# Two attention blocks, forward and backward on one core: how O, dQ, dwo and dwq work is placed, in which order stores are issued, and how the first head's K is transposed

## The chip, the cores and the metric

The kernel runs on one core of a Trainium2 chip. A core has TensorE (matmuls, and transposes done as matmuls against an identity), VectorE, ScalarE, GpSimd and SyncE, each with an instruction queue of its own, and DMA queues. The metric is the time of one execution on the device in microseconds (us).

## The reference

Two independent attention blocks, A and B, get the same shapes: batch 8, 96 queries, 32 heads of 128, 512 cached keys and values, model width 640. The program returns the forward result and all gradients, in bf16:

```python
q = (x @ wq).reshape(B, Sq, H, Dh)          # B=8 Sq=96 D=640 H=32 Dh=128
scores = einsum("bhqd,bhkd->bhqk", q, k_cache) * Dh ** -0.5      # Sk=512
o = einsum("bhqk,bhkd->bhqd", softmax(scores), v_cache)
out = o.reshape(B, Sq, H * Dh) @ wo         # of A and of B, side by side
# reference() returns out and the gradients of x, k_cache, v_cache, wq, wo of both blocks
```

With P the softmax and O the head's output, the backward pass needs per head: dO = g wo^T, dV = P^T dO, dP = dO V^T, dS = P (dP - rowsum(O dO)), dK = dS^T Q, dQ = dS K, dwo = O^T g, dwq = x^T dQ, dx = dQ wq^T.

## The kernel before

The work is cut into **ticks**. Each block has 32 heads, each head 8 batch elements, and each (head, batch element) pair starts one tick after the one before; so a head takes 8 ticks, a block 256. `build_block` (line 54) adds closures to an `Emitter` (line 16) with a tick and a slot; `Emitter.run` sorts them by tick, slot and order of adding, and calls them. That gives the program order. The framework's scheduler may still move an instruction ahead or back within its engine's queue, by readiness as it reckons it and by program order as priority. An instruction that goes through `pinned` (line 111) stays behind the one that was traced before it on its engine.

In what follows an offset is counted in ticks from a pair's own first tick (`ct`), or from its head's first tick (`c0t`).

**A pair's stages** (table `OFF`, line 45). K and V come from memory for two batch elements at a time, on SyncE's queue (`c_ld`, lines 262 to 270). V is transposed by DMA (`c_xt`, line 275). K is transposed by DMA for the batch elements 2, 3, 6, 7 (two at a time, issued at offset -3) and on TensorE for 0, 1, 4, 5 (`c_s1`, line 280, at offset 2: four transposes and a VectorE copy to `KT_pe`); `k_on_pe` (line 548) chooses. At offset 3 the scores S and their row maximum (lines 298, 300), the exponential on ScalarE (line 310), the reciprocal (line 320) and, on GpSimd, P = E / sum (`P_sb`, line 329, pinned). At offset 4 the transposes of P into the bank `x_ps` (line 365) and dV (line 389), evacuated by ScalarE (line 392). At 5 O^T (line 359), evacuated to the tile `OD` (line 375), and on GpSimd O * dO (`prod`, line 407, pinned). At 6 dP and the row sums `dl_ps` (lines 417, 419), then dS on VectorE (line 421). At 7 the transposes of dS (line 346) and dK (line 432), evacuated by ScalarE (line 435). At 8 dQ^T (line 340).

**Stores** of dV and dK go out on GpSimd's queue for two batch elements together (`c_st`, line 395; the issue is line 398), one tick after the second one's evacuation, in a slot behind P_sb and prod of that tick. They are not pinned. The tiles `dV_sb` and `dK_sb` have three buffers each.

**A head's own work** is placed by the table `HK` (line 46): transposes of wo and wq (`pB`), the projections Q^T and dO^T (`pC`), their transposes back (`pD`), and after the pairs:

- `qA` (line 438): transposes of O^T (which = 0) and dQ^T (which = 1) into `Onat` and `dQnat`, six each, evacuated by VectorE; O at offset 18, dQ at 17
- `qB` (line 459): dwo in two halves of 320 columns, six matmuls each (line 470), offsets 19 and 20, evacuated by ScalarE to `dwo_sb`; with the second half the store is issued on GpSimd's queue (line 474)
- `qD` (line 477): dwq for two heads at a time, with the odd one, in five blocks of 128 rows and 6 matmuls of 256 columns each (line 490); two blocks share a bank and a VectorE evacuation at offsets 18 and 19, the fifth comes at 21; the store of `dwq_sb` is line 496

`Onat`, `dQnat`, `dwo_sb` and `dwq_sb` have one buffer each. O^T and dQ^T of the last eight heads lie in `OD`. The last head of the second block has offsets of its own.

**A group's work**: for every five or six heads `gU` (line 501) adds their share of out and of dx, spread over some nine ticks each; line 512 has its matmuls.

**Between the blocks**: the second block's x and gradient are loaded in 12 pieces (`setup_ld`, line 114, pinned on SyncE's queue), through a pool of five buffers. The last seven can be loaded only when an earlier piece has been transposed (`setup_T`, line 122) and its buffer is free; they are transposed themselves in ticks -4 to -1 of the second block. They are loaded again in natural layout (`setup_nat`, line 138) for dwo and dwq, from ticks 13 (gradient) and 15 (x), into the tiles that the first block's dwo and dwq still read until then.

Of the kernel before, what the change touches and what calls it, by code (L numbers as in the profile page):

```python
# [13 lines left out]


class Emitter:
    def __init__(self):
        self.items = []
        self.n = 0

    def add(self, tick, slot, fn):
        self.items.append((tick, slot, self.n, fn))
        self.n += 1

    def run(self):
        self.items.sort(key=lambda x: (x[0], x[1], x[2]))
# [14 lines left out]
SL_HEAD = 90  # L41
SL_GRP = 95
SL_SETUP = 96

OFF = dict(ldk=-5, ldv=-3, kt=-3, vt=0, s2=3, s3=3, s4=4, s5=5, s6=6, s7=7, s8=8)
HK = dict(pA=-10, pA2=-9, pB=-3, pC0=[-2, 0], pC1=[-1, 0], pD1=1, pD0=2, qA0=18, qA1=17, qB=[19, 20], qD=[(18, 0, 2), (19, 2, 4), (21, 4, 5)])
EV = dict(pB0="act", pB1="dve", pC00="act", pC01="act", pC10="act", pC11="dve", pD0="dve", pD1="dve", qA0="dve", qA1="dve", qB0="act", qB1="act", qD="dve", gU="act")
GSPREAD0 = 9
PRIO_OFF = 2000
# [4 lines left out]
def build_block(tc, em, tick0, blk, x, kc, vc, wq, wo, g_all, out_all, dx, dk, dv, dwq, dwo, ident, ones, pools, HG=6, first=True, groups=None):  # L54
    nc = tc.nc
# [116 lines left out]
    if first:  # L172
        for which_, tk in ((0, -12), (1, -11)):
            em.add(tick0 + tk, SL_LOAD + which_, setup_nat(which_, 0, 4))
            em.add(tick0 + tk, SL_LOAD + which_, setup_nat(which_, 4, TT))
    else:
        for which_, tk in ((1, 13), (0, 15)):
            for i, t in enumerate(range(0, TT, 2)):
                em.add(tick0 + tk + i // 2, SL_LOAD, setup_nat(which_, t, min(t + 2, TT)))

# [99 lines left out]
    def c_s1(h, b):  # L280
        def f():
            st = CS[(blk, h, b)]
            kT_ps = bank([128, Sk], BF16, "kT_ps")
            for c in range(KC):
                nc.tensor.transpose(kT_ps[:, c * 128:(c + 1) * 128], st["K_sb"][:, c, :], ident[:])  # L285
            KT = wk.tile([128, Sk], BF16, name="KT_pe", bufs=2)
            nc.vector.tensor_copy(KT[:], kT_ps[:])
            st["KT"] = KT[:]
        return f
# [105 lines left out]
    def c_st(h, b, which):  # L395
        def f():
            dst = dv if which == "v" else dk
            nc.gpsimd.dma_start(dst[b - 1:b + 1, h].rearrange("b (p c) d -> p b (c d)", c=KC), SB.pop((blk, h, b // 2, which))[:])  # L398
        return f

    def c_s5b(h, b):
# [144 lines left out]
    NTS = len(tsplits)  # L546

    def k_on_pe(h, b):
        return (b // NB) % 2 == 0

    SX = pools["SX"]
    for g in range(NG):
        h0 = GH0[g]
        for hh in range(groups[g]):
            h = h0 + hh
            c0t = tick0 + h * B
            if not (first and h == 0):
                em.add(c0t + HK["pA"], 54.6, pA(h))
                em.add(c0t + HK["pA2"], 54.6, pA2(h))
            em.add(c0t + HK["pB"], SL_HEAD, pB(h))  # L560
            fh = first and h == 0
            for si in range(NTS):
                em.add(c0t + HK["pC0"][min(si, len(HK["pC0"]) - 1)], SL_HEAD, pC(h, 0, si))
                em.add(c0t + (3 if fh else HK["pC1"][min(si, len(HK["pC1"]) - 1)]), SL_HEAD + (7 if fh else 0), pC(h, 1, si))
            em.add(c0t + (3 if fh else HK["pD1"]), SL_HEAD + (8 if fh else 0), pD(h, 1))
            em.add(c0t + (4 if fh else HK["pD0"]), SL_HEAD, pD(h, 0))
            for b in range(B):
                ct = c0t + b
                if b % NB == 0:
                    em.add(tick0 - 12 if first and h == 0 and b == 0 else ct + OFF["ldk"], SLOTS["LOAD"], c_ld(h, b, "K", 7))  # L570
                    em.add(ct + OFF["ldv"], SLOTS["LOAD"], c_ld(h, b, "V", 5))
                    if not k_on_pe(h, b):
                        em.add(ct + OFF["kt"], SLOTS["LOAD"] + 1, c_xt(h, b, "KT", 2))
                    em.add(ct + OFF["vt"], SLOTS["LOAD"] + 1, c_xt(h, b, "VT", 4))
                if k_on_pe(h, b):
                    em.add(ct + 2, SLOTS["S1"], c_s1(h, b))
                em.add(ct + OFF["s2"], SLOTS["S2A"], c_s2a(h, b))
                em.add(ct + OFF["s2"], SLOTS["S2B"], c_s2b(h, b))
                em.add(ct + OFF["s3"], SLOTS["S3A"], c_s3a(h, b))
                em.add(ct + OFF["s3"], SLOTS["S3B"], c_s3b(h, b))  # L580
                em.add(ct + OFF["s5"], SLOTS["S5B"], c_s5b(h, b))
                if b % 2 == 1:
                    em.add(ct + OFF["s4"] + 1, 54.3, c_st(h, b, "v"))
                    em.add(ct + OFF["s7"] + 1, 54.3, c_st(h, b, "k"))
                em.add(ct + OFF["s4"], SLOTS["S4"], c_s4(h, b))
                for i, o in enumerate(("s8", "s7", "s5", "s4")):
                    SX.setdefault(ct + OFF[o], [None] * 4)[i] = (blk, h, b)
                em.add(ct + OFF["s6"], SLOTS["S6"], c_s6(h, b))
                em.add(ct + OFF["s7"], SLOTS["S7"], c_s7(h, b))
            hk = HK if first or h < H - 1 else dict(HK, qA0=13, qB=[14, 15], qA1=16, qD=[(19, 0, 2), (19, 2, 4), (19, 4, 5)])  # L590
            em.add(c0t + hk["qA0"], SL_HEAD, qA(h, 0))
            for di in range(len(wsplits)):
                em.add(c0t + hk["qB"][di], SL_HEAD + 1, qB(h, di))
            em.add(c0t + hk["qA1"], SL_HEAD, qA(h, 1))
            for (k_, c_lo, c_hi) in hk["qD"]:
                if c_lo < DC and h % 2 == 1:
                    em.add(c0t + k_, SL_HEAD + 2, qD(h, c_lo, min(c_hi, DC)))
        cLg = tick0 + (h0 + groups[g] - 1) * B + B - 1
        gs0 = max(3, (GSPREAD0 * groups[g]) // HG)
        gs1 = max(3, (GSPREAD1 * groups[g]) // HG)  # L600
        if not first and g == NG - 2:
            gs0, gs1 = 9, 9
        if g == 0:
            em.add(cLg + OFF["s5"] - 2, SL_LOAD, setup_acc)
        subs = [(0, t, gi) for t in range(TT) for gi in range(len(gsplits))] + [(1, t, gi) for t in range(TT) for gi in range(len(gsplits))]
        n_out = TT * len(gsplits)
        for i, (which, t, gi) in enumerate(subs):
            if which == 0:
                tk = cLg + OFF["s5"] + 2 + (i * gs0) // n_out
            else:  # L610
                tk = cLg + OFF["s8"] + 2 + gs0 - 3 + ((i - n_out) * gs1) // n_out
            em.add(tk, SL_GRP, gU(g, which, t, gi))
    pools["c_s45"] = c_s45
    pools["c_s8"] = c_s8
    return tick0 + H * B
# [2 lines left out]
def _kernel_impl(tc, A_x, A_k_cache, A_v_cache, A_wq, A_wo, B_x, B_k_cache, B_v_cache, B_wq, B_wo, grad_out,  # L618
# [13 lines left out]
    with ExitStack() as ctx:  # L632
# [36 lines left out]
        for tk, (k8, k7, k5, k4) in pools["SX"].items():  # L669
            em.add(tk, SLOTS["S8"], pools["c_s8"](tk, k8, k7))  # L670
            em.add(tk, SLOTS["S5"], pools["c_s45"](tk, k8, k5, k4))
        em.run()


# [62 lines left out]
```

## Time and profile before

| | |
|---|---|
| median of 5 runs | 1716.59 us (1706.99 to 1733.63) |
| profiled execution | 1706.99 us, span 1705.2 us |
| TensorE matmul / weight load busy | 1678.3 us (98%) / 1341.7 us (79%) |
| VectorE / ScalarE / GpSimd busy | 1321.9 (78%) / 1381.9 (81%) / 1046.5 us (61%) |
| DMA | 424.66 MB, mean 249 GB/s |
| mean granted TensorE clock | 0.998 of full |

The page comes from one execution. The span runs from the first to the last instruction; the execution's own time is 1.8 us more. A row of a group has the line, the engine, the operation, the tiles written and read, and the count; then the time busy, the mean of one in ns, and the idle time of the engine just before, with what ended it. A row of waits has who waited for whom, then the total, the number and the longest in us. A row of the timeline has start and duration in us, and in square brackets the idle time before and its releaser. A row of windows has the stretch, its length, and then the busy time of each engine with its instructions in brackets; behind that the granted TensorE clock, the DMA share (the packets' time over 16 engines' time, which goes over 1 where packets wait in line) and GB/s. A matmul's end is modelled, so a wait below some 0.2 us can be missing from the idle time.

### The profile page before, as it was taken

What the parts mean: (1) busy time and instruction counts of PE and PEld (TensorE: products, weight loads), DVE (VectorE), ACT (ScalarE), POOL (GpSimd) and SP (SyncE); (2) the same over time, 40 slices, a digit from 0 to 9 for tenths busy, and PEclk for the clock granted to TensorE, in tenths of its full rate; (3) what the DMA queues carried; (4) which work ended last, traced back from release to release, by engine and by line L of the source; (5) the groups of instructions that cost most, each with busy time, mean ns of one, the idle gap of its engine ahead of it and who ended that gap; (6) DMA issues with size and microseconds to landing.
All of it is one profiled execution on the core that took longest, in us unless ns stands there. A gap on an engine that the chain in (4) does not pass through costs nothing.

```text
span 1705.2 us, 57281 instructions
## 1 busy us (share of the span) xinstructions
PE 1678.3 (98%) x21976; PEld 1341.7 (79%) x21976; DVE 1321.9 (78%) x3040; ACT 1381.9 (81%) x3518; POOL 1046.5 (61%) x1747
## 2 busy tenths in 40 slices
PE   8999999999999999999899999999999999999999
PEld 7787778778878778878678777887788778778876
DVE  6787678778778878788778776787788788778777
ACT  7899799778869869869768897897799679868974
POOL 4676466556657657657566665675577557656754
PEclk9999999999999999999999999999999999999999
DMA  9999999989999999999999999999999999989994
GB/s 268 252 269 274 253 235 283 254 198 262 245 234 249 263 235 253 250 250 269 261 255 245 276 274 243 250 243 262 235 266 259 243 227 271 282 199 246 262 233 132
DMA packets 606770, 424.66 MB, mean 249 GB/s; under 512 B 425696, under 2 KB 564320, under 8 KB 606496
## 3 DMA queue, kind: packets, MB, share of 16 engines
q1 hardware_dynamic: 552912, 243.65, 72.4%
q0 software_dynamic: 53584, 177.35, 31.7%
q8 instruction: 172, 2.82, 0.7%
q14 instruction: 102, 0.84, 0.2%
HBM read 161.09 MB, written 159.12 MB: 188 GB/s over the span
## 4 chain that ended last, share of the span: by engine, by line
PE 89%; DMA 4%; ACT 2%; POOL 2%; issue 2%; DVE 1%; DVEq 0%; SPq 0%; POOLq 0%; ACTq 0%
PE o_ps L512 12%; PE q_ps L243 12%; PE dK_ps L432 6%; PE dV_ps L389 6%; PE S_ps L298 6%; PE dwq_ps L490 6%; PE dP_ps L417 6%; PE dwo_ps L470 6%; PE x_ps L365 5%; PE x_ps L340 5%; PE dst_ps L346 5%; PE x_ps L359 5%; PE kT_ps L285 3%; PE n_ps L258 3%; PE nat_ps L455 3%; DMA KT<-K_sb 2%
## 5 line engine op out<-in xcount | busy, mean ns | idle before, releaser
L329 POOL TENSOR_SCALAR P_sb<-E_sb,rinv 96x512 bf16<-96x512 bf16 x512 | 352.0, 688 | 379.6 <-DVE rinv L320 369.9
L310 ACT ACTIVATE E_sb<-S_ps,negm 96x512 bf16<-96x512 f32 x512 | 354.9, 693 | 210.0 <-DVE negm L300 197.8
L421 DVE SCALAR_TENSOR_TENSOR dS_sb<-dP_ps,dl_ps,P_sb 96x512 bf16<-96x512 f32 x512 | 383.1, 748 | 65.4 <-PE dl_ps L419 49.1
L300 DVE TENSOR_REDUCE negm<-S_ps 96x1 f32<-96x512 f32 x512 | 347.7, 679 | 55.1 <-PE S_ps L298 51.8
L435 ACT ACTIVATE dK_sb<-dK_ps 128x512 bf16<-128x512 f32 x512 | 307.0, 600 | 67.2 <-PE dK_ps L432 62.6
L392 ACT ACTIVATE dV_sb<-dV_ps 128x512 bf16<-128x512 f32 x512 | 316.2, 618 | 0.0
L398 POOL DMA_DIRECT2D out_dram<-dV_sb x256 | 193.7, 757 | 134.3 <-ACT dV_sb L392 125.3
L378 ACT ACTIVATE PT_sb<-x_ps 128x384 bf16<-128x384 bf16 x512 | 257.7, 503 | 1.1 <-PE x_ps L365 1.1
L398 POOL DMA_DIRECT2D out_dram<-dK_sb x256 | 192.6, 752 | 84.3 <-ACT dK_sb L435 53.7
L512 PEld LDWEIGHTS <-OD 128*128 128x128 bf16 x1536 | 132.1, 98 | 99.8 <-issue 0.2
L389 PE MATMUL dV_ps<-dOnat_h,P_sb 96*128 96x128 bf16 x2048 | 198.2, 219 | 1.0 <-DVE dOnat_h L160 0.8
L417 PE MATMUL dP_ps<-VT,dOT_h 128*96 128x512 bf16 x512 | 195.5, 382 | 2.9 <-DMA VT<-V_sb 2.8
L432 PE MATMUL dK_ps<-Qnat_h,dS_sb 96*128 96x128 bf16 x2048 | 197.9, 219 | 0.0
L407 POOL TENSOR_TENSOR prod<-OD,dOT_h 128x96 bf16<-128x96 bf16 x512 | 186.0, 363 | 9.1 <-ACT OD L375 5.2
L348 DVE COPY dST_sb<-dst_ps 128x384 bf16<-128x384 bf16 x512 | 177.3, 346 | 9.2 <-PE dst_ps L346 7.9
L320 DVE RECIPROCAL rinv<-rowsum 96x1 f32<-96x1 f32 x512 | 79.5, 155 | 125.4 <-ACT E_sb L310 119.8
L365 PE MATMUL x_ps<-ident,P_sb 96*128 96x96 bf16 x2048 | 172.3, 205 | 4.3 <-POOL P_sb L329 3.1
L375 ACT ACTIVATE OD<-x_ps 128x192 bf16<-128x192 f32 (+1 forms) x515 | 172.5, 335 | 4.4 <-PE x_ps L340 3.8
L359 PE MATMUL x_ps<-PT_sb,V_sb 128*128 128x96 bf16 x2048 | 172.1, 206 | 0.4 <-ACT PT_sb L378 0.4
L346 PE MATMUL dst_ps<-ident,dS_sb 96*128 96x96 bf16 x2048 | 172.0, 206 | 0.5 <-DVE dS_sb L421 0.5
L340 PE MATMUL x_ps<-dST_sb,K_sb 128*128 128x96 bf16 x2048 | 170.6, 206 | 0.4 <-ACT PT_sb L378 0.4
L340 PEld LDWEIGHTS <-K_sb 128*128 128x128 bf16 x2048 | 131.5, 98 | 25.1 <-issue 1.0
(83 smaller groups left out, 3717.7 us busy)
## 6 DMA issues: line engine op xcount, KB each, us to landing
out_dram<-dV_sb POOLq DMA_DIRECT2D x256, 256.0 KB, 5.0
out_dram<-dK_sb POOLq DMA_DIRECT2D x256, 256.0 KB, 5.0
K_sb<-in_A_k_cache_dram SPq DMA_DIRECT2D x128, 256.0 KB, 5.2
V_sb<-in_A_v_cache_dram SPq DMA_DIRECT2D x128, 256.0 KB, 5.0
K_sb<-in_B_k_cache_dram SPq DMA_DIRECT2D x128, 256.0 KB, 4.8
V_sb<-in_B_v_cache_dram SPq DMA_DIRECT2D x128, 256.0 KB, 5.1
out_dram<-dwo_sb POOLq DMA_DIRECT2D x63, 160.0 KB, 4.9
out_dram<-dwq_sb POOLq DMA_DIRECT2D x31, 320.0 KB, 5.8
```

The costliest lines, as they stand in the source:

```text
L300: nc.vector.tensor_reduce(negm[:], S_ps[:], axis=AX.X, op=ALU.max, negate=True)
L310: nc.scalar.activation(E_sb[:], st["S_ps"][:], ACT.Exp, bias=st["negm"][:], scale=1.0, accum_out=rowsum[:])
L329: pinned(nc.gpsimd.tensor_scalar(P_sb[:], st["E_sb"][:], st["rinv"][:], 0.0, op0=ALU.mult, op1=ALU.add))
L340: nc.tensor.matmul(dQT_ps, st["K_sb"][:, c, :], st["dST_sb"][:, c * Sq:(c + 1) * Sq], start=(c == 0), stop=(c == KC - 1))
L389: nc.tensor.matmul(dV_ps[:, c * 128:(c + 1) * 128], P_sb[:, c * 128:(c + 1) * 128], hs["dOnat_h"][:, b * 128:(b + 1) * 128], start=True, s ...
L392: nc.scalar.activation(SB[(blk, h, b // 2, "v")][:, b % 2], dV_ps[:], ACT.Identity, scale=1.0)
L398: nc.gpsimd.dma_start(dst[b - 1:b + 1, h].rearrange("b (p c) d -> p b (c d)", c=KC), SB.pop((blk, h, b // 2, which))[:])
L417: nc.tensor.matmul(dP_ps[:], hs["dOT_h"][:, tok], st["VT"], start=True, stop=True)
L421: nc.vector.scalar_tensor_tensor(dS_sb[:], dP_ps[:], dl_ps[:, 0:1], st["P_sb"][:], op0=ALU.subtract, op1=ALU.mult)
L432: nc.tensor.matmul(dK_ps[:, c * 128:(c + 1) * 128], dS_sb[:, c * 128:(c + 1) * 128], hs["Qnat_h"][:, b * 128:(b + 1) * 128], start=True, s ...
L435: nc.scalar.activation(SB[(blk, h, b // 2, "k")][:, b % 2], dK_ps[:], ACT.Identity, scale=1.0)
L512: nc.tensor.matmul(o_ps[:], src[:, t * 128:(t + 1) * 128], rhs, start=(hh == 0), stop=(hh == groups[g] - 1))
```

## The change

The emitter gets a second way to add work. `later` takes an earliest and a latest tick, a slot, a number of TensorE columns and a gap (the least number of ticks behind the entry before it); entries keep their order in one chain over both blocks. All other work is booked with its columns per tick. `place` first gives every entry its earliest possible tick, then goes backward through the chain, up to 60 times, and moves an entry between its neighbours to the tick that lowers the sum of squared columns most; it stops when nothing moves.

The transposes `qA`, the halves of `qB` and the blocks of `qD` of all heads go through `later`, but for the last two heads of the second block, which keep fixed offsets. In the chain an odd head's work follows the even head's: O transposes, dwo halves, and with the odd head both dQ transposes and then dwq in five pieces, each with a bank and an evacuation of its own. An entry may be up to 58 ticks behind its head's first tick; the first block's work must end by tick 14 of the second block. The natural-layout loads of the second block move from ticks 13 and 15 to 15 and 17, and its dwo begins no earlier than tick 19.

The stores of dV and dK are pinned. For the first head of the first block all eight K go through TensorE, and its two transposing DMAs of K are left out.

```diff
 class Emitter:
...
-    def add(self, tick, slot, fn):
+    def add(self, tick, slot, fn, cols=0):
         self.items.append((tick, slot, self.n, fn))
         self.n += 1
+        self.cols[tick] = self.cols.get(tick, 0) + cols
+
+    def later(self, lo, hi, slot, fn, cols, gap=0):
+        self.chain.append([lo, hi, slot, fn, cols, gap])
+
+    def place(self):
+        ch = self.chain
+        at = []
+        for i, (lo, hi, _, _, cols, gap) in enumerate(ch):
+            t = max(lo, at[-1] + gap) if at else lo
+            at.append(t)
+            self.cols[t] = self.cols.get(t, 0) + cols
...
+        for _ in range(60):
+            moved = False
+            for i in reversed(range(len(ch))):
+                lo, hi, _, _, cols, gap = ch[i]
+                a = max(lo, at[i - 1] + gap) if i else lo
+                z = min(hi, at[i + 1] - ch[i + 1][5]) if i + 1 < len(ch) else hi
+                best, bt = 0, at[i]
+                for t in range(a, z + 1):
+                    if t != at[i]:
+                        d = (self.cols.get(t, 0) + cols) ** 2 + (self.cols[at[i]] - cols) ** 2 - self.cols.get(t, 0) ** 2 - self.cols[at[i]] ** 2
+                        if d < best:
+                            best, bt = d, t
+                if bt != at[i]:
+                    self.cols[at[i]] -= cols
+                    self.cols[bt] = self.cols.get(bt, 0) + cols
+                    at[i] = bt
+                    moved = True
+            if not moved:
+                break
+        for t, (_, _, slot, fn, _, _) in zip(at, ch):
+            self.add(t, slot, fn)
...
+QHOLD = 58
+QEND = 14
+QPIECES = [(0, 1), (1, 2), (2, 3), (3, 4), (4, 5)]
...
-        for which_, tk in ((1, 13), (0, 15)):
+        for which_, tk in ((1, 15), (0, 17)):
...
-            nc.gpsimd.dma_start(dst[b - 1:b + 1, h].rearrange("b (p c) d -> p b (c d)", c=KC), SB.pop((blk, h, b // 2, which))[:])
+            pinned(nc.gpsimd.dma_start(dst[b - 1:b + 1, h].rearrange("b (p c) d -> p b (c d)", c=KC), SB.pop((blk, h, b // 2, which))[:]))
...
-        return (b // NB) % 2 == 0
+        return (b // NB) % 2 == 0 or (first and h == 0)
...
-            hk = HK if first or h < H - 1 else dict(HK, qA0=13, qB=[14, 15], qA1=16, qD=[(19, 0, 2), (19, 2, 4), (19, 4, 5)])
...
+            if first or h < H - 2:
+                end = tick0 + H * B + (QEND if first else -8 + 9)
+                dl = min(c0t + QHOLD, end)
+                em.later(c0t + 13, dl, SL_HEAD, qA(h, 0), T)
+                for di, (_, w) in enumerate(wsplits):
+                    em.later(max(c0t + 14, tick0 + 19), dl, SL_HEAD + 1, qB(h, di), TT * w, 1 if di == 0 else 0)
+                if h % 2 == 1:
+                    em.later(c0t + 16, dl, SL_HEAD, qA(h - 1, 1), T)
+                    em.later(c0t + 16, dl, SL_HEAD, qA(h, 1), T)
+                    for i, (c_lo, c_hi) in enumerate(QPIECES):
+                        em.later(max(c0t + 17, tick0 + 21), min(c0t + QHOLD + 8, end), SL_HEAD + 2, qD(h, c_lo, c_hi), (c_hi - c_lo) * TT * 256, 1 if i == 0 else 0)
+            else:
+                qa0, qb, qa1, qd = (13, (14, 15), 16, 19) if h == H - 1 else (18, (19, 20), 17, None)
...
+        em.place()
         em.run()
```

## The prediction

> **What bounds the kernel now.** I read the engine table of the page first, then the idle time of TensorE by stretch, then the waits, then the places where a wait was longest. The page's first, clock and DMA rows:
>
> ```profile
> span 1705.2 us, 57281 instructions
> ...
> PE 1678.3 (98%) x21976; PEld 1341.7 (79%) x21976; DVE 1321.9 (78%) x3040; ACT 1381.9 (81%) x3518; POOL 1046.5 (61%) x1747
> ...
> PEclk9999999999999999999999999999999999999999
> DMA  9999999989999999999999999999999999989994
> ```
>
> TensorE is idle for 1705.2 - 1678.3 = 26.9 us in all. Everything that better placement can win lies in that idle time, in waits too short to show as idle (a matmul's modelled end covers about 0.2 us), and in half-clock stretches. The same idle time by stretch, from the windows (length, then TensorE's busy time; clock and DMA share at the end):
>
> ```profile
> 0.00:42.00 42.00, 36.78 (x464) 29.89 (x465) 26.39 (x62) 31.31 (x74) 18.94 (x37) 1.00 1.05 271
> 42.00:85.00 43.00, 40.10 (x529) 32.47 (x530) 31.97 (x76) 36.27 (x95) 27.66 (x47) 0.96 1.13 249
> 85.00:300.00 215.00, 213.34 (x2840) 171.78 (x2839) 162.36 (x370) 189.13 (x484) 139.02 (x231) 1.00 1.09 262
> 300.00:800.00 500.00, 498.87 (x6540) 397.80 (x6539) 398.99 (x923) 402.59 (x1030) 308.39 (x514) 1.00 1.06 247
> 800.00:860.00 60.00, 54.46 (x719) 43.90 (x718) 44.08 (x104) 42.64 (x110) 33.34 (x57) 0.97 1.08 267
> 860.00:1660.00 800.00, 793.50 (x10429) 635.56 (x10428) 624.59 (x1432) 658.13 (x1676) 500.12 (x834) 1.00 1.06 251
> ```
>
> Start 5.2, next 43 us 2.9, the border between the two blocks 5.5, and 9.3 in the 1,515 us of steady heads (1.7 + 1.1 + 6.5). The planner's work is in that last part, where TensorE hardly waits.
>
> What it waits for there is P_sb, made by GpSimd. From the waits (total, times, longest):
>
> ```profile
> POOL out_dram L398 <- ACT dV_sb L392: 128.3, 235, 1.9
> ...
> POOL out_dram L398 <- ACT dK_sb L435: 55.5, 45, 3.2
> ...
> PEld L365 <- POOL P_sb L329: 8.5, 29, 1.4
> ```
>
> The rows of line 365 put 11.6 us of idle time, 34 times, on P_sb (weight load and matmul records together). One of the longest, in the timeline:
>
> ```profile
> 1577.67 0.72 POOL L398 DMA_DIRECT2D out_dram<-dK_sb  x1 [1.93 <-ACT dV_sb L392]
> 1578.43 0.70 POOL L329 TENSOR_SCALAR P_sb<-E_sb,rinv 96x512 bf16<-96x512 bf16 x1
> ...
> 1579.19 0.30 PE L365 MATMUL x_ps<-ident,P_sb 96*128 96x96 bf16 x3 [1.21 <-POOL P_sb L329]
> ```
>
> A store stands in GpSimd's queue before its data exist, GpSimd waits 1.93 us, P_sb comes behind the store, TensorE loses 1.2. Of the 48 starts at line 365 that come over 60 ns late in the trace (11.0 us in sum), 39 (8.0 us) follow a P_sb that started directly behind a dK store.
>
> **The change, part by part**, against the profiled execution: span 1705.2, 1.8 around it, 1706.99. That is the fastest of five runs (median 1716.59, highest 1733.63); I carry the difference over to the median.
>
> *Stores in program order.* Today a store may move ahead in GpSimd's queue. Pinned, the order in a tick is P_sb, prod, store, and each store's data were evacuated one tick earlier (dV at offset 4, store at 5; dK at 7, store at 8), so it should find them ready. The 8.0 us go; what can come back is a P_sb of the next tick behind the late 0.75 us issue. GpSimd's tick is 0.69 + 0.36 + 0.75 = 1.8 us, and light ticks (41 planned at 5,000 to 5,500 columns) took 2.46 on average, so mostly not. Behind a pinned store stand P_sb, prod, the loads of wo and wq (lines 190, 199) and the pinned chain after them; TensorE and dS wait for those. I take -6; ends -11.6 (all waits on P_sb) and +8 (the same stall moved behind the dV stores). The three output buffers of dV and dK cover a store landing 5.0 us after issue: three pairs of ticks are over 15 us.
>
> *Placement.* I worked the rule through on the matmuls' column counts. All matmuls together have 3,788,800 columns, and from first to last start of the trace that is 1,700 us, 0.449 ns a column. Per tick the plan before runs from 4,936 to 12,360 columns (standard deviation 1,834 over ticks 30 to 519); after it 4,936 to 11,848, deviation 1,783. Over three neighbouring ticks the deviation goes up, from 1,394 to 1,555: each move shifts one entry between its neighbours in the chain, and stops early. Ticks under 6,000 columns go from 132 to 150. So the change levels little. The framework's scheduler does some of it already: the 24 ticks planned at 4,500 to 5,000 columns held 6,065 on average in the trace (counted between successive S matmuls) and took 2.81 us. With 9.3 us idle in the steady part, most of it counted above, I take -1; ends -5 and +5 (the idle time left, gained or once more).
>
> [...]
>
> *dwq in five pieces.* The same 30 matmuls a pair of heads. VectorE evacuates 5 x 0.414 = 2.07 us instead of 2 x 0.688 + 0.414 = 1.79 (rows by form): 0.28 x 31 pairs = 9 us of VectorE, 78% busy with 383 us idle, spread over the run. I cost it at 0; if the cover fails, up to +4 (half of it). Five banks a pair instead of three, eight in all: in the same bound.
>
> *dwo buffer.* dwo_sb has one buffer. Before, heads follow each other at 8 ticks. After, in 16 of 31 pairs the odd head's first piece comes 2 ticks after the even head's last (5,704 + 8,648 columns x 0.449 = 6.4 us; a few have more). ScalarE may not overwrite the buffer before the store has landed. Counting each store from the start of the last evacuation before it to its landing, I get 2.5 to 7.9 us, median 5.7; 22 of 64 exceed 6.4, mean excess over all 0.22. From the rows of dwo_sb, the store alone:
>
> ```profile
> DMA to landing us min/median/max: 1.9/4.9/7.1
> ```
>
> So ScalarE stops for about 16 x 0.22 = 3.5 us. Queued behind are E_sb, OD, PT_sb, the dV and dK evacuations, and TensorE waits for these; PT_sb is ready 1.1 us before its matmul in the median. I take +1; ends 0 and 16 x 1.5 = +24.
>
> *K of the first head on TensorE.* Four more groups of four transposes and four copies; 2,048 columns x 0.449 = 0.9 us. The copies are 4 x 0.408 = 1.6 us of VectorE, which has 15.6 us free in the first 42. Two transposing DMAs go (SyncE was busy issuing them for 2.25 and 1.24 us), and with them loads come earlier; but no TensorE wait there after the first x load ends on a transposing DMA. +1; upper end +3.2 (four groups of 0.39 plus the copies, all exposed). Lower end: the wait for VT at 77.85 us goes as the DMA backlog shrinks:
>
> ```profile
> 77.85 0.39 PE L417 MATMUL dP_ps<-VT,dOT_h 128*96 128x512 bf16 x1 [2.82 <-DMA VT<-V_sb]
> ```
>
> and the window around it:
>
> ```profile
> 76.00:84.00 8.00, 6.15 (x62) 4.96 (x63) 3.96 (x9) 2.21 (x7) 2.16 (x4) 0.79 1.04 244
> ```
>
> The clock fell to 0.79 of full over 8 us, another 0.21 x 8 = 1.7 us, so -4.5 at most. The Trainium skill ("TensorE: Matmul & The Clock Gate", Part 1) has the clock halve after an idle window of about 3.4 us; by that the 2.8 us wait would have cost itself alone, and the lower end would be -2.8. The row shows the loss after 2.8, so it decides.
>
> *Border of the blocks.* The last pieces of the second block's x and gradient must wait for a free buffer, so that they are loaded some two ticks ahead of their transposes, and the waits there end on these DMAs (5.5 us idle, 0.03 x 60 = 1.8 us of clock). In ticks -5 to -3 of the second block the plan drops from 21,208 to 15,832 columns, 2.4 us less cover. +1.5; ends +5 (2.4 and one more half-clock stretch with a remainder) and -7.3 (all of it gone). The natural-layout loads move by two ticks: g_nat is issued from tick 15 to 17 and first used at 19; ticks 17 and 18 hold 8,648 and 8,392 columns, 7.6 us, against 5.7 to landing. 0; up to +2. SyncE's queue behind them holds K and V loads, due five ticks later.
>
> Sum: -6 - 1 + 0 + 1 + 1 + 1.5 = -3.5 us: 1703.5 for an execution like the profiled one, **1713 us** against the median.
>
> **Rivals.**
> 1. *Faster.* All P_sb waits go (11.6), the VT wait with its clock (4.5), the border's (7.3), less 1.0 for the added transposes: -22, 1694. For it: each cause is in the trace. Against: the two DMA waits have other causes than those edits, with the DMA share at 1.05 to 1.13 throughout.
> 2. *Slower.* The dwo store lands late and ScalarE stands in 16 pairs for the longest time seen: +24, with -6, +1, +1.5 of the other terms about +20, 1737. It decides once landing takes over about 7.5 us from the evacuation (1.1 of slack above 6.4) in most of those pairs. For it: 22 of 64 pass 6.4 already, GpSimd's queue now holds every store in order ahead of it, and ScalarE works in order. Against: few pass 7.5, and the scheduler may send later work ahead.
> 3. *It does not level, and nothing moves.* The scheduler places these matmuls as before, and pinned stores trade one wait for another: within 3 us, 1716. The poor levelling worked out above speaks for it; the 39 late P_sb against. It ends in the same class as my forecast, and they share a chance.
>
> **Numbers.** My forecast with rival 3: 0.65. Faster by over 1% (17 us, which is also about what a measurement of this kernel can tell from no change): 0.19, all of rival 1. Slower by over 1%: 0.16, rival 2 with less or more of its price. The distances of the ends from the values, added as squares, are 12.5 down and 28.5 up from 1713; the upper one is nearly all dwo buffer, for which all 16 pairs would have to be at the longest landing. With the rivals at 1694 and 1737 I give 1695 to 1735, which leaves out the last of rival 1 and the far half of rival 2, under 2 in 10.
>
> **What would show it.** Right: GpSimd's stores no longer wait for dV_sb (128 us now) or dK_sb (56), line 365's idle time under 5 us. TensorE's idle in 300 to 800 us stays near 1 us: levelling had nothing to win. ScalarE's waits gain a row "dwo_sb <- DMA out_dram<-dwo_sb" of a few us. VectorE's busy time up by some 9 us, 16 more kT_ps transposes. Wrong: a row of tens of us for dwo_sb; line 365's waits unchanged; idle over 9 us at the border; or a total that moved by 17 us without any of these rows.

## The result and the profile after

The changed kernel takes 1721.97 us in the median (1712.54 to 1738.16, 43 runs), the kernel before 1718.0 us beside it (1701.56 to 1737.13, 80 runs). The ratio is 1.0042, 95% interval 1.0027 to 1.0056: 7 us slower, where I had forecast 3.5 us faster. (Ratios leave disturbed executions of both kernels out, so they aren't the quotient of the medians.)

The profiled execution took 1722.91 us, 15.9 more than that of before. That one was among the fastest of its kernel (1706.99 for a median of 1718.0), so the two traces lie further apart than the medians. The page after, first rows, clock and DMA:

```profile
span 1721.1 us, 56844 instructions
...
PE 1689.8 (98%) x21992; PEld 1344.6 (78%) x21992; DVE 1333.4 (77%) x3106; ACT 1378.6 (80%) x3518; POOL 1037.2 (60%) x1747
...
PEclk9999999999999999999999999999999999999999
DMA  9999999989999999989999999999899999999994
```

TensorE is idle for 31.3 us instead of 26.9. Its busy time grew by 11.5 us for 16 more matmuls: matmuls run into each other, and where one comes late by less than the modelled end of the one before, that shows as busy. By stretch, from the windows after (length, then TensorE's busy time; clock and DMA share at the end):

```profile
300.00:800.00 500.00, 494.87 (x6420) 392.61 (x6417) 396.13 (x926) 394.73 (x1008) 298.82 (x503) 1.00 1.03 243
800.00:860.00 60.00, 55.29 (x755) 45.78 (x754) 45.68 (x109) 46.25 (x121) 35.31 (x60) 0.97 1.10 269
860.00:1660.00 800.00, 793.00 (x10336) 630.56 (x10334) 622.94 (x1450) 652.69 (x1667) 495.24 (x833) 1.00 1.06 250
```

From 300 to 800 us TensorE is idle for 5.1 us instead of 1.1, and it got through 120 matmuls fewer in the same time (6,420 for 6,540). So the steady heads became slower, the part in which I had found nothing to win or lose. The border of the blocks, 800 to 860, is as before: 4.7 us idle (5.5), clock 0.97.

The waits after:

```profile
ACT dwo_sb L201 <- DMA out_dram<-dwo_sb: 11.0, 6, 3.5
...
PEld L409 <- POOL P_sb L373: 8.3, 29, 1.0
...
PE dl_ps L463 <- ACT dwo_sb L201: 3.6, 4, 2.2
...
POOL out_dram L442 <- ACT dK_sb L479: 2.4, 1, 2.4
```

GpSimd's stores no longer wait: the row for dV_sb (128.3 us before) is gone, dK_sb fell from 55.5 to 2.4. Yet TensorE waits for P_sb as long as before, 29 times, 8.3 us (8.5). The row of dwo_sb that I had named is there with 11.0 us, and 3.6 us of it reach TensorE.

**A finer measure.** Idle time hides short waits, so I also counted **late starts**: matmul records that begin over 60 ns later than the usual spacing behind a matmul of that many columns, between 70 and 1650 us, by what ended the wait; gaps of exactly one missing record (0.216 us for 512 columns) left out, since most traces from x1_fixO on lack some 150 to 165 of the 21,992 matmul records. Those that no DMA ended come to 25.6 us before and 40.5 us after, +14.9. Those that a DMA ended fell from 13.4 to 7.2 us. (The expectations ahead of z3_chain2w still have the missing records in: 28.2 and 46.2. Their bounds are held against the counts without them.)

The growth is not behind P_sb: that sum is 9.3 us before and 10.2 after. Sorted by the engine that ended them, with a usual spacing set slightly shorter (28.1 and 44.6 us in all), the late starts behind ScalarE go from 7.5 to 30.3 us, behind GpSimd from 9.7 to 10.4, behind VectorE from 9.7 to 3.7. The largest new ones are the projections' matmuls (q_ps) behind the exponential (5.5 us), S matmuls behind the dK evacuation (5.4), matmuls into x_ps behind the evacuation PT_sb (5.0, 1.4 before) and the row sums (dl_ps) behind dwo_sb (4.4).

Where the late starts stand led to the later runs. I put each to its tick, and the ticks (30 to 499) into classes by planned columns:

| planned columns of the tick | before: ticks, late us | after: ticks, late us |
|---|---|---|
| under 6,000 | 124, 9.1 | 141, 25.8 |
| 6,000 to 7,000 | 168, 11.6 | 108, 3.8 |
| 7,000 to 8,000 | 12, 0.0 | 52, 1.0 |
| 8,000 to 9,000 | 20, 0.5 | 57, 4.8 |
| 9,000 and more | 146, 4.4 | 112, 3.6 |

The growth stands mostly in the **light ticks**. How much of it depends on where one tick is cut from the next: cut in front of the S matmul, the first two rows come to 5.6 and 13.4 us before and 14.9 and 13.7 after; cut in front of the transposes of P, to 13.6 and 7.2 before and 26.3 and 2.8 after. What happens in a light tick shows in the timeline after, at a late P_sb:

```profile
308.34 0.60 ACT L479 ACTIVATE dK_sb<-dK_ps 128x512 bf16<-128x512 f32 x1 [0.50 <-PE dK_ps L476]
...
308.83 0.67 ACT L354 ACTIVATE E_sb<-S_ps,negm 96x512 bf16<-96x512 f32 x1
...
309.47 0.74 DVE L465 SCALAR_TENSOR_TENSOR dS_sb<-dP_ps,dl_ps,P_sb 96x512 bf16<-96x512 f32 x1
...
310.13 0.15 DVE L364 RECIPROCAL rinv<-rowsum 96x1 f32<-96x1 f32 x1
...
310.39 0.68 POOL L373 TENSOR_SCALAR P_sb<-E_sb,rinv 96x512 bf16<-96x512 bf16 x1 [2.06 <-DVE rinv L364]
...
311.12 0.20 PEld L409 LDWEIGHTS <-P_sb 96*128 96x128 bf16 x4 [0.27 <-POOL P_sb L373]
```

No store stands in front of P_sb here; GpSimd had been free for 2.06 us. The chain dK evacuation, exponential, reciprocal (behind dS on VectorE), P_sb takes 308.34 to 311.07, 2.7 us. In that time TensorE ran out of other work. Of the late starts behind P_sb after the change (10.2 us), 40 (8.5 us) follow a P_sb that itself waited for rinv; before, 37 (7.1 us of 9.3) followed a P_sb directly behind a store.

### The profile page after: what moved, and what is told of

It is laid out like the page before. It is cut to its first block, busy times and chain, and to the rows that moved or that the text cites. A ratio compares the mean times of both kernels' runs of the same rounds, so it can differ in the third digit from the quotient of the medians.

```text
span 1721.1 us, 56844 instructions
## 1 busy us (share of the span) xinstructions
PE 1689.8 (98%) x21992; PEld 1344.6 (78%) x21992; DVE 1333.4 (77%) x3106; ACT 1378.6 (80%) x3518; POOL 1037.2 (60%) x1747
## 4 chain that ended last, share of the span: by engine, by line
PE 64%; ACT 18%; issue 8%; POOL 3%; DMA 3%; DVE 3%; ACTq 0%; SPq 0%; DVEq 0%; POOLq 0%
PE o_ps L556 12%; PE q_ps L287 9%; PE dwo_ps L514 6%; ACT E_sb L354 6%; PE dwq_ps L534 4%; PE S_ps L342 4%; PE dK_ps L476 4%; PE dV_ps L433 4%; PE dP_ps L461 4%; ACT dK_sb L479 4%; ACT dV_sb L436 3%; PE x_ps L409 3%; PE dst_ps L390 3%; PE x_ps L384 3%; ACT PT_sb L422 3%
## 5 line engine op out<-in xcount | busy, mean ns | idle before, releaser
L384 PEld LDWEIGHTS <-K_sb 128*128 128x128 bf16 x2048 | 130.8, 98 | 22.8 <-issue 4.5
```

Of the source, the lines that this page charges most:

```text
L384: nc.tensor.matmul(dQT_ps, st["K_sb"][:, c, :], st["dST_sb"][:, c * Sq:(c + 1) * Sq], start=(c == 0), stop=(c == KC - 1))
```

## The experiments

All were timed beside the kernel before, which is what the ratios are to. Each figure of late starts is from one trace.

| kernel | ratio, 95% interval | late starts, no DMA (behind P_sb) |
|---|---|---|
| before | 1 | 25.6 (9.3) |
| changed kernel | 1.0042 [1.0027, 1.0056] | 40.5 (10.2) |
| e1_pin: pins alone | 0.9993 [0.9950, 1.0035] | 24.4 (3.4) |
| e2_place: placement alone | 1.0057 [1.0022, 1.0091] | 37.6 (12.0) |
| e3_k: K alone | 0.9982 [0.9950, 1.0015] | 23.3 (9.6) |
| x4_pink: pins and K | 0.9976 [0.9937, 1.0015] | 24.6 (3.8) |
| e4_dwo2: changed, two dwo buffers | 1.0030 [0.9999, 1.0061] | 37.2 (10.0) |
| x3_dve: changed, dwo evacuated by VectorE | 1.0039 [1.0008, 1.0070] | 48.1 (9.0) |
| y2_pieces: changed, dwq in three pieces | 1.0020 [0.9991, 1.0050] | 40.7 (11.1) |
| x1_fixO: O and dwo at fixed ticks | 0.9973 [0.9939, 1.0007] | 26.9 (3.6) |
| x2_fixQ, x2_again: dQ and dwq at fixed ticks | 0.9919 [0.9886, 0.9953], 0.9967 [0.9934, 1.0001] | 19.4 (3.9), 19.5 (3.8) |
| y4_x2nopin: x2_fixQ without pins | 0.9968 [0.9935, 1.0002] | 23.3 (9.5) |
| y1_two: two chains | 0.9971 [0.9938, 1.0003] | 28.3 (9.6) |
| y5_start4: one chain, later start | 0.9982 [0.9947, 1.0018] | 40.9 (9.4) |
| z3_chain2w: two chains, two-tick search | 1.0138 [1.0087, 1.0190] | 50.2 (0.5) |
| z4_three: one chain, three-tick search | 1.0074 [1.0038, 1.0109] | 46.0 (2.6) |
| z3_dwo2: z3_chain2w, two dwo buffers | **0.9866** [0.9831, 0.9901] | 19.1 (0.5) |
| z4_dwo2: z4_three, two dwo buffers | 0.9930 [0.9899, 0.9960] | 28.5 (2.6) |
| z6_nopin: z3_dwo2 without pins | 0.9967 [0.9936, 0.9998] | 24.3 (0.9) |

**The parts, one at a time.** e1_pin is the kernel before with

```diff
-            nc.gpsimd.dma_start(dst[b - 1:b + 1, h].rearrange("b (p c) d -> p b (c d)", c=KC), SB.pop((blk, h, b // 2, which))[:])
+            pinned(nc.gpsimd.dma_start(dst[b - 1:b + 1, h].rearrange("b (p c) d -> p b (c d)", c=KC), SB.pop((blk, h, b // 2, which))[:]))
```

> The kernel before with the stores of dV and dK pinned, nothing else; the order of the other queues is that of the kernel before, so that only GpSimd's order differs. Theory of the prediction: the 39 late P_sb behind a dK store (8.0 us in the trace of before) go, the time falls by 3 to 8 us (ratio 0.995 to 0.998). Rival (a pinned store costs as much as it saves): ratio 0.999 to 1.002, and the late starts of line 365 stay near 11 us. Rival (pinning is what made the changed kernel slower): ratio 1.003 or more.

e2_place is the changed kernel with this taken back, and `k_on_pe` too (the natural-layout loads keep their two ticks):

> The changed kernel without the pinned stores and without the first head's K on TensorE: the placement alone. Theory A (the placement makes new waits, for PSUM banks and for the dwo buffer): slower than before by 7 to 15 us (ratio 1.004 to 1.009), with the new waits of the changed kernel in its trace: S matmuls behind O transposes that wait for the dK evacuation (5.4 us there), q_ps behind dl_ps (4.4), n_ps (3.0), dl_ps behind a dwo evacuation (4.5). Rival (the placement is neutral, one of the two others costs): ratio 0.998 to 1.002.

e3_k is the kernel before with

```diff
-        return (b // NB) % 2 == 0
+        return (b // NB) % 2 == 0 or (first and h == 0)
```

> The kernel before with all K of the first head on TensorE, nothing else. Theory of the prediction: +1 us (ratio 1.0000 to 1.0015), and the wait for VT near 78 us may or may not be there. Rival (the start is what made it slower): +4 us or more, with more idle time of TensorE in the first 42 us.

x4_pink has both of these edits and no placement:

> The kernel before with the pinned stores and the first head's K on TensorE, without the placement. Theory (the placement alone is the loss): ratio 0.995 to 1.000, late P_sb at line 365 under 6 us, and regular waits otherwise as in the kernel before. Rival (the parts only cost together): ratio over 1.002.

The loss is the placement's: alone it gives 1.0057. K does nothing that can be measured. The pins do in e1_pin what they were to do, in its waits:

```profile
POOL out_dram L398 <- ACT dK_sb L435: 2.4, 1, 2.4
...
PEld L365 <- POOL P_sb L329: 2.2, 8, 0.6
```

Line 365's wait falls from 8.5 to 2.2, the late starts behind P_sb from 9.3 to 3.4. But all late starts that no DMA ended fall by 1.2 only: `dl_ps` comes late by 2.0 us more, and once TensorE stands 3.2 us because ScalarE waited 3.3 us for a dK_sb buffer whose store hadn't landed. Late starts that a DMA ended rose by 5.8 (13.4 to 19.2). The time stayed.

**The dwo buffer and what evacuates it.** e4_dwo2 and x3_dve are the changed kernel with one edit each,

```diff
-                st["dwo_sb"] = hd.tile([128, D], BF16, name="dwo_sb", bufs=1)
+                st["dwo_sb"] = hd.tile([128, D], BF16, name="dwo_sb", bufs=2)
```

and, in the table `EV`, `qB0="dve", qB1="dve"` in the place of `"act"`, for x3_dve.

> The changed kernel with two buffers for dwo_sb; all queues keep the changed kernel's order. Theory B (the dwo buffer is the cause): the waits of ScalarE for the dwo store (11.0 us, 6 times) go and with them the 4.5 us of TensorE behind them; ratio to the kernel before falls from 1.0042 to 0.999 to 1.001. Theory A (mostly PSUM banks): those waits go, but the ratio stays at 1.001 to 1.004 and the waits for banks stay.

> The changed kernel with dwo evacuated by VectorE instead of ScalarE (128 evacuations, ScalarE's take 0.44 us each). If the new waits come from ScalarE's queue in the ticks where dwo and Q, dO evacuations meet: the late starts that no DMA ended fall by 8 us or more, ratio under 1.001. If they come from the PSUM banks whoever empties them, or VectorE pays as much: no change or more, ratio 1.002 to 1.008.

With two buffers the late starts behind dwo_sb (4.5 us, 5 times) go and all others stay; the ratio's interval overlaps the changed kernel's. With VectorE the wait moves: `dl_ps` then comes late behind VectorE's dwo_sb, 9 times, 10.5 us. So the buffer is a small part of this loss, and taking dwo off ScalarE gains nothing.

**Half of the placement undone.** x1_fixO and x2_fixQ are the changed kernel with one kind of work back at the offsets of before:

```diff
-                em.later(c0t + 13, dl, SL_HEAD, qA(h, 0), T)
+                em.add(c0t + 18, SL_HEAD, qA(h, 0), T)
                 for di, (_, w) in enumerate(wsplits):
-                    em.later(max(c0t + 14, tick0 + 19), dl, SL_HEAD + 1, qB(h, di), TT * w, 1 if di == 0 else 0)
+                    em.add(c0t + 19 + di, SL_HEAD + 1, qB(h, di), TT * w)
```
```diff
-                    em.later(c0t + 16, dl, SL_HEAD, qA(h - 1, 1), T)
-                    em.later(c0t + 16, dl, SL_HEAD, qA(h, 1), T)
-                    for i, (c_lo, c_hi) in enumerate(QPIECES):
-                        em.later(max(c0t + 17, tick0 + 21), min(c0t + QHOLD + 8, end), SL_HEAD + 2, qD(h, c_lo, c_hi), (c_hi - c_lo) * TT * 256, 1 if i == 0 else 0)
+                    for k_, c_lo, c_hi in ((18, 0, 2), (19, 2, 4), (21, 4, 5)):
+                        em.add(c0t + k_, SL_HEAD + 2, qD(h, c_lo, c_hi), (c_hi - c_lo) * TT * 256)
```

In the second each head also gets `qA(h, 1)` at offset 17.

> The changed kernel with the O transposes and the dwo halves back at the fixed offsets 18, 19 and 20 of every head; dQ and dwq stay with the planner. In the steady ticks the matmul starts that come over 60 ns late and are not ended by a DMA sum to 31 us before and 50 us in the changed kernel. Theory C (O and dwo of the odd head now fall on the ticks in which the next head's wo, wq, Q and dO work holds PSUM banks and ScalarE): the sum falls to 25 to 35 us, the S matmuls behind O transposes (5.4 us) and q_ps behind dl_ps (4.4) go, ratio 0.997 to 1.001. Rival (dQ and dwq in five pieces are the cause): it stays at 42 us or more, ratio 1.003 or more.

> The changed kernel with the dQ transposes and dwq back at their fixed offsets (17; 18, 19, 21, two blocks of dwq to a bank); O and dwo stay with the planner. Theory C: the late starts that no DMA ended stay at 42 us or more, ratio 1.002 to 1.006. Rival (dQ and dwq are the cause): they fall to 25 to 35 us, ratio 0.997 to 1.001.

Both theories that blamed one half fell: x1_fixO came out as theory C said, but x2_fixQ against it. Either half undone takes the loss away, and x2_fixQ is faster than the kernel before. Neither kind of work costs when moved by itself. Working the planner's rule through gave the next theory: with all in one chain, an entry can only move between its neighbours; the deviation over three ticks is 1,556 columns in the changed kernel, 1,280 and 1,315 in these two.

**Is it the unevenness of the plan?** y1_two gives the two kinds a chain each:

```diff
-        self.chain = []
+        self.chains = ([], [])
...
-    def later(self, lo, hi, slot, fn, cols, gap=0):
-        self.chain.append([lo, hi, slot, fn, cols, gap])
+    def later(self, lo, hi, slot, fn, cols, gap=0, c=0):
+        self.chains[c].append([lo, hi, slot, fn, cols, gap])
```

y5_start4 keeps one chain and begins each entry later:

```diff
-            t = max(lo, at[-1] + gap) if at else lo
+            lo = max(lo, at[-1] + gap) if at else lo
+            t = max(lo, min(ch[i][0] + 4, top[i]))
```

y2_pieces has `QPIECES = [(0, 2), (2, 4), (4, 5)]`; y4_x2nopin is x2_fixQ without the pins.

> The same entries and bounds, in two chains, O with dwo and dQ with dwq; each entry now moves between neighbours of its own kind. Plan: deviation of the columns per tick 1,456 (changed kernel 1,783), over three neighbouring ticks 1,281 (1,556). Theory L (the single chain gets stuck and leaves heavy ticks where heads change; the level of the plan is what costs): ratio to the kernel before 0.990 to 0.998, and matmul starts over 60 ns late that no DMA ended, between 70 and 1650 us, at or under 32 us (changed kernel 46.2, before 28.2). Rival M (moving both kinds off their fixed ticks at once is what costs, wherever they go): ratio 1.001 or more, late starts over 40 us.

> The changed kernel with its one chain; only the first position of each entry is four ticks later than its earliest one (as far as its latest one allows), so that the search starts with room on both sides. Plan: 1,568 per tick, 1,280 over three ticks. Theory L: ratio 0.990 to 0.998, late starts not ended by a DMA at or under 32 us, as with two chains. Rival M (both kinds moved is what costs): ratio 1.001 or more. If two chains are fast and this one is not, it is the order of the two kinds within one chain, not the level of the plan.

> The changed kernel with dwq in three pieces again (two blocks a bank), one chain as in the changed kernel. Plan as uneven as the changed kernel's: 1,850 per tick, 1,564 over three. Theory L: ratio 1.001 to 1.008, late starts not ended by a DMA over 38 us. Rival P (the five pieces, with five banks and five VectorE evacuations a pair of heads, are what costs): ratio 0.999 or less, late starts under 32 us.

> The kernel with dQ and dwq at fixed ticks (ratio 0.9919), its stores unpinned again. Theory: pinned stores save the waits on P_sb (5.3 us with, some 11 us without), and with a level plan this shows in the time: ratio 0.994 to 0.998, 4 to 6 us over the pinned one, with P_sb late starts of 9 us or more. Rival: the pinning earns nothing in the time here either, as when it was made alone (0.9993): ratio 0.990 to 0.993.

y1_two came out as theory L said, y5_start4 just outside its bound in time and far outside it in late starts (40.9). The pieces aren't the cause. y4_x2nopin came out as its theory said (0.9968, and 9.5 us behind P_sb again), but x2_again, below, gave 0.9967 with the pins in: that they are worth something in the time here is not shown.

**Plans more even than these.** In the search, z3_chain2w (on y1_two) and z4_three (on y5_start4) count two and three ticks together; here for two:

```diff
-                            d = (self.cols.get(t, 0) + cols) ** 2 + (self.cols[at[i]] - cols) ** 2 - self.cols.get(t, 0) ** 2 - self.cols[at[i]] ** 2
+                            ws = {x for u in (t, at[i]) for x in range(u - 1, u + 1)}
+                            d = -sum(sum(self.cols.get(x + j, 0) for j in range(2)) ** 2 for x in ws)
+                            self.cols[t] = self.cols.get(t, 0) + cols
+                            self.cols[at[i]] -= cols
+                            d += sum(sum(self.cols.get(x + j, 0) for j in range(2)) ** 2 for x in ws)
+                            self.cols[t] -= cols
+                            self.cols[at[i]] += cols
```

> Two chains, and the search lowers the squared columns of two neighbouring ticks together instead of one tick's. Plan: 1,420 per tick, 1,100 over three ticks, 61 ticks under 6,000 columns (changed kernel 1,783, 1,556, 148). Theory L (the unevenness, above all the light ticks, is the cost): ratio 0.988 to 0.995, late starts not ended by a DMA at or under 24 us between 70 and 1650 us (missing records left out; changed kernel 40.5, two chains 28.3). Rival M (moving both kinds costs by itself): ratio 0.996 to 1.002, late starts 28 us or more.

> One chain as in the changed kernel, first positions four ticks later, and the search lowers the squared columns of three neighbouring ticks. Plan: 1,530 per tick, 977 over three ticks, 87 ticks under 6,000 columns. Theory L by three ticks: ratio 0.988 to 0.995, late starts at or under 26 us. Theory L by single light ticks: between two chains (85 light ticks, 0.9971) and the fixed dQ and dwq (0.9919). Rival M: ratio 0.997 or more, as with the later start alone (0.9982).

> The kernel with dQ and dwq at fixed ticks once more, on the same chip as the two others: ratio 0.989 to 0.995 if its 0.9919 holds; late starts not ended by a DMA 17 to 22 us.

By theory L alone z3_chain2w and z4_three had to be the fastest; they are the slowest of all. x2_again missed the range expected of it (0.9967); its interval overlaps that of x2_fixQ, and its late starts are the same. The waits of z3_chain2w say what happened:

```profile
ACT dwo_sb L207 <- DMA out_dram<-dwo_sb: 27.2, 8, 5.1
...
PE dwq_ps L540 <- ACT dwo_sb L207: 17.7, 7, 3.9
...
PEld L415 <- POOL P_sb L379: 1.6, 6, 0.5
```

P_sb is settled: 1.6 us instead of 8.3, and 3.8 us of late starts in ticks under 6,000 columns instead of 25.8. But ScalarE stands 27.2 us before dwo_sb. One of the eight places in the timeline:

```profile
1104.54 0.44 ACT L207 ACTIVATE dwo_sb<-dwo_ps 128x320 bf16<-128x320 f32 x1 [4.53 <-DMA out_dram<-dwo_sb]
...
1105.03 1.60 PE L540 MATMUL dwq_ps<-dQnat,x_nat 128*128 128x256 bf16 x7 [3.92 <-ACT dwo_sb L207]
```

and the windows around it:

```profile
1101.00:1105.00 4.00, 0.11 (x2) 0.04 (x1) 0.00 (x0) 0.46 (x2) 0.00 (x0) 1.00 1.31 110
1105.00:1108.00 3.00, 2.97 (x15) 2.05 (x15) 1.89 (x4) 2.33 (x7) 1.75 (x3) 0.52 0.35 128
```

Nearly every engine stands for 4 us, and then TensorE runs at 0.52 of its clock for 3. From one head's last dwo evacuation to the next head's first there were 19.3 us in the kernel before, mostly; in the changed kernel 6.1 to 8.1 us in 14 pairs; here 3.7 to 5.9 us in a dozen, the waits included (with the second buffer, below, 2.7 to 4.5 in 15). A store takes 1.9 to 8.1 us from issue to landing, 4.7 in the median (rows of the tile dwo_sb).

**Both causes removed.** z3_dwo2 and z4_dwo2 add the second dwo buffer to these two. Every queue holds the same instructions in the same order.

> The kernel with two chains and two-tick search, with two buffers for dwo_sb; every queue holds the same instructions in the same order. Theory B2 (the one buffer is what the even plan pays with): ScalarE's wait for the store of dwo_sb gone (27.2 us before), late starts not ended by a DMA at or under 30 us (50.2 before, 22.8 of them behind dwo_sb), at most three half-clock stretches (seven before), ratio 0.984 to 0.994. Rival (the even plan costs by itself and the store is only where it shows): ratio 1.003 or more.

> The kernel with one chain and three-tick search, with two buffers for dwo_sb, all queues in the same order. Theory B2: ScalarE's wait for the store gone (18.7 us before), late starts not ended by a DMA at or under 34 us (46.0 before, 13.5 of them behind dwo_sb), ratio 0.988 to 0.999 (1.0074 before). Rival: ratio 1.003 or more.

```profile
span 1694.5 us, 56894 instructions
...
PE 1671.3 (99%) x21992; PEld 1341.4 (79%) x21992; DVE 1337.9 (79%) x3106; ACT 1386.4 (82%) x3518; POOL 1038.7 (61%) x1747
```

This is the page of z3_dwo2: 40.6 us less span than the same order with one buffer, of which its profile had shown 27.2 us of waiting before dwo_sb (22.8 us as late starts) and seven half-clock stretches, now two. The median falls from 1734.74 to 1696.41 us. With a ratio of 0.9866 it beats the kernel before by 23 us and, by the two ratios, the changed kernel by 30 us. In the uneven plan the same edit gave 1.0042 to 1.0030. With two buffers in each, e4_dwo2, z4_dwo2 and z3_dwo2 differ in the plan alone, and their intervals (0.9999 to 1.0061, 0.9899 to 0.9960, 0.9831 to 0.9901) hardly touch: the plan costs by itself, and a single chain is not what costs. So the plan and the buffer were two prices of which the changed kernel paid mainly the first, z3_chain2w mainly the second.

**The pins again.** z6_nopin is z3_dwo2 with the stores unpinned.

> The fastest kernel (two chains, two-tick search, two buffers for dwo_sb; ratio 0.9866) with the stores of dV and dK not pinned. Theory: the waits on P_sb come back as they were before the change (late starts behind P_sb 5 to 10 us instead of 0.5) and cost their sum: ratio 0.989 to 0.993. Rival: an unpinned store costs nothing that lasts, since other waits shrink by as much: ratio 0.984 to 0.988.

Neither expectation holds: late starts behind P_sb stay at 0.9, and yet the ratio is 0.9967, 1% over z3_dwo2. Its waits show another place:

```profile
PE S_ps L348 <- DMA KT<-K_sb: 15.6, 5, 6.5
...
PEld L348 <- DMA KT<-K_sb: 8.7, 3, 3.8
```

Late starts that a DMA ended are 23.8 us instead of 7.9. That the order of the stores is what makes transposed K late is not shown: e1_pin, with pinned stores, has such waits too (19.2 us). The two kernels were timed apart, each beside its own runs of the kernel before (medians 1720.17 and 1720.48).

## Why the prediction was wrong

The time, 1722 us, lies in the range that I gave, but by luck: the upper half of that range was nearly all the dwo buffer, and what made the kernel slower was the placement, to which I had given a gain.

**Placement, −1 with ends −5 and +5: the step that failed.** It measured +0.57% by itself, some 10 us, and in its best form, with the buffer, the pins and K, some −23 us. I had worked out that the deviation over three ticks rises from 1,394 to 1,555 and that ticks under 6,000 columns go from 132 to 150 (worked through again: 1,387 to 1,556, and 130 to 148), and then priced both at nothing, because TensorE is idle for 9.3 us only in the steady heads. Two things were wrong with that bound. The waits are mostly shorter than what idle time shows: 25.6 us of late starts where no DMA is involved. And idle time left bounds neither what levelling can win (z3_dwo2 won 23 us, the pins and K included, where 9.3 were idle) nor what a worse plan can lose. The trace of before would have shown where TensorE waits (20.7 of its 25.6 us lay in ticks under 7,000 columns), but not the price: the changed kernel has 17 more ticks under 6,000 columns and 60 fewer up to 7,000, which at before's 0.07 us a tick would come to 3 us less (an estimate from the table). What rose is the wait per light tick, from 0.07 to 0.18 us. In the plan the light ticks stand closer (ticks 30 to 499): before there are 40 alone and 42 twos, in the changed kernel none alone, 42 twos and 19 threes. Two neighbouring ticks hold under 12,000 columns together 114 times before, 156 times in the changed kernel, 141 in y2_pieces, 55 to 94 in x1, x2, y1 and y5, 34 and 37 in the plans of z3 and z4. No run tests this measure by itself.

That the unevenness of the plan is the cause within the placement rests on x1, x2 and y1 (levelled, faster), and on e4_dwo2, z4_dwo2 and z3_dwo2. No one number of the plan orders all runs: x2_fixQ has more light ticks than y1_two (108 and 85 of ticks 30 to 519) and fewer late starts (19.4 and 28.3). And over three ticks the plan of y5_start4 is as even as that of y1_two (1,280 and 1,281; by single ticks 1,568 and 1,456), yet it has 40.9 us of late starts. Some 8.4 of them stand behind dwo_sb, for which its ScalarE waited 14.0 us; the rest, 32.5, is still above y1_two's 28.3.

**dwo buffer, +1 with ends 0 and +24.** Right in mechanism, too small in size: ScalarE stood 11.0 us for the 3.5 that I had counted, and 4.5 us of late starts went with the second buffer; in the time that is 1.0042 to 1.0030, with intervals that overlap. Rival 2 had the right mechanism for a case I didn't see: an evener plan packs the heads' dwo closer (2.7 us without the wait, instead of the 6.4 I counted with) and the landing time, whose median I had about right (4.9; 4.7 there), then decides. There it cost 38 us, beyond its upper end: 22.8 us of late starts, and a half-clock stretch with five of the eight waits.

**Stores, −6.** The waits of the stores went as said, and alone the pins took 5.9 us off the late starts behind P_sb. Two parts of the step failed. P_sb stayed as late in the changed kernel, for a new reason (rinv in light ticks). And without placement the gain didn't reach the time: 0.9993. The bound "the same stall moved behind the dV stores" isn't what came back; waits on dl_ps, on one dK_sb buffer and on DMAs are; that the pins brought those on DMAs is not shown. That three buffers cover the landing of a store failed once, for 3.3 us.

**dwq in five pieces, 0**: y2_pieces can't be told from the changed kernel. VectorE's busy time rose by 11.5 us (9 said, and 1.6 for K). **K, +1**: 0.9982, nothing measurable; from 42 to 85 us TensorE is idle for 0.3 us after the change (2.9 before) and the clock is at 1.00 (0.96), the lower end that I had given, but in e1_pin, without the K edit, the half-clock stretch near 79 us is missing too. **Border, +1.5**: 4.7 us idle for 5.5, clock unchanged; at most −1. **Natural-layout loads, 0**: no wait on them stands out.

**Rival 1**, −22: the VT wait went, the border stayed, P_sb stayed. **Rival 3** named the poor levelling, but not its price.

The Trainium skill ("Perfetto Trace Analysis", Identifying the Most-Contended Engine) has TensorE's headroom judged by the share of peak arithmetic and by the weight loads' busy share, not by the busy share of matmuls. Here the weight loads' share stayed at 79% between the kernel before and z3_dwo2, while 23 us went. The late starts show part of them: 6.5 us fewer where no DMA is involved and 5.5 fewer behind DMAs.

One thing stays open. Over the executions behind the ratios, a straight line per kernel through time and mean granted clock (common slope 2.8 us for 0.001) puts the changed kernel 11.8 us above the kernel before at the same clock; its mean clock is higher, 0.9978 against 0.9961, which gives 4.8 back. Placement alone has the same 0.9978, pins alone 0.9958. Fewer waits on DMAs in the traces (7.2 and 5.7 us for 13.4) go with it. What makes the DMAs meet their matmuls better in these kernels wasn't settled.

## What to carry to other kernels

Idle time alone is no bound for a change of placement: before a planner moves work, put the late starts of the trace against the planned load of their ticks, and look at the lightest ticks, above all where they stand together and the chain of the other engines is longer than the matmuls that cover it. When work of one kind is moved closer together, count its output buffers against the time from issue to landing of their stores at the new distance, not the old one. And test levelling and buffering together: here the buffer alone gave 1.0030 and the two-tick levelling alone 1.0138, both together the fastest version (0.9866).

## What the runs showed of the hardware

- A wait of TensorE of 4.0 us was followed by 3 us at 0.52 of the clock (windows above). In the traces of four kernels (before, after, z3_chain2w, z6_nopin) all 12 matmuls that came over 2.5 us late have a stretch of 3.4 us or more at a lower clock that begins in the wait or within 1.9 us after it, and so do 4 of the 14 that came 1.2 to 2.5 us late (one of 1.5 us). The Trainium skill ("TensorE: Matmul & The Clock Gate", Part 1) names an idle window of about 3.4 us; here shorter waits do it too, so a wait of 1.5 to 3 us may cost more than itself.
- The spread of each kernel from execution to execution goes along with the granted clock, by the 2.8 us for 0.001 given above.
